# k's first loads on another queue, the first pair's roots on ScalarE and VectorE, the third pair's squares on VectorE

## The chip, the cores and the metric

The kernel runs on one core of a Trainium2 chip. The metric is the device time of one execution in microseconds, the median of the runs made. The engines are TensorE (PE, with its weight loads as PEld), VectorE (DVE), ScalarE (ACT), GpSimd (POOL) and SyncE (SP), which issues most of the loads and stores.

## The reference, cut to what matters

Attention over 8 batches of 12 heads with 448 positions of 64 features, q and k normalised by their root mean square and a gain, then a feed-forward block with a squared ReLU. All data are float32.

```python
def rmsnorm(x, g):
    rms = np.sqrt(np.mean(x * x, axis=-1, keepdims=True) + 1e-06)
    return x / rms * g
q_n, k_n = (rmsnorm(q, g_q), rmsnorm(k, g_k))
scores = 1.0 / np.sqrt(q.shape[-1]) * np.matmul(q_n, k_n.transpose(0, 1, 3, 2))
scores = scores - np.max(scores, axis=-1, keepdims=True)
attn = np.exp(scores)
attn = attn / (np.sum(attn, axis=-1, keepdims=True) + 1e-09)
x = np.matmul(attn, v).transpose(0, 2, 1, 3).reshape(B * S, H * D)
h = x @ w_in
return np.maximum(h, 0.0) ** 2 @ w_out
```

## The kernel before

The heads are taken in pairs, 48 of them. The first twelve pairs are computed alone (`attention_alone`), while the weights of the feed-forward block are read and prepared beside them by VectorE, ScalarE and POOL (`weights`, one small step at a time); after that, attention of later pairs is woven into the matmuls of the feed-forward block. The order of the instructions on each engine is the order in which the program writes them (a manual schedule): every engine runs its own list in order, and waits at an instruction until what it needs is there. No scheduler moves anything. SP likewise issues its transfers in the order of the program, and holds all later ones while it waits for the place of one to come free.

The tile `qk` has eight places of 512 columns, four for the pairs of even number and four for the odd ones. q and k of a pair lie as 112 rows of 4 x 2 x 64 numbers, in two of the four (`places_of`). The other two take the squares. Two pairs later q and k go to one place that held q and to one that held the squares of k.

Each pair of heads needs the reciprocal root of the mean square of each row of q and of k. `normalise_in_turn` does it for the first three pairs, q first and then k: square (L333, ScalarE), sum over 64 columns (L334, VectorE), mean and small constant (L335, VectorE), power of minus one half (L336, POOL). q is then multiplied by its root (L339, VectorE). k isn't: k's roots are the factors of the exponentials later (L820), one per row. For the later pairs `norm` and `roots` do q and k in one, with a logarithm and an exponential on ScalarE (L742, L743) and one Newton step, three small operations on VectorE (L744 to L746), in place of the power.

`first_pair` stands ahead of all. It issues the loads of q (L316, SP), of two small rows of gains (L1588, SP), of k in two loads (L326, SP), and of the gains in columns (L364, POOL), then q and k of the second pair (SP). Ahead of it the table of ScalarE's functions is loaded (L1606). VectorE clears a tile (L377), TensorE runs three matmuls on it (L380) while nothing else is there, and `normalise_in_turn` follows. Between q's and k's part stand the small operations on the gains (`between`: L1591 to L1593, and L373, which multiplies the two gains). TensorE transposes k and q (L385); ScalarE copies k (L387) and scales q by the gains (L389). From L1593 a bound is read by all engines and a branch taken (L1609, L1612); the branch of the whole row maximum isn't taken with these inputs.

In `attention_alone` the first step is: scores of the first pair (L816), exponentials (L820), transposes of the second pair between them (L791, copied at L793 and scaled at L795), first sum (L833), norm of the third pair (`norm(2)`), v of the second pair, first values (L879), load of the fourth pair. Before it stand `load(2)`, two loads of weights (L545) and `norm(1)`. The preparation of the weights has L594 and L611 on ScalarE, L608, L613 and L618 on VectorE, L580 and L588 on POOL. Each scores' matmul needs a bank that the exponentials of the one before left.

Of the kernel before, what the change touches and what calls it, by code (L numbers as in the profile page):

```python
# [10 lines left out]
F32 = mybir.dt.float32  # L11
U32 = mybir.dt.uint32
AF = mybir.ActivationFunctionType
ALU = mybir.AluOpType
# [290 lines left out]
def places_of(qk, i, work):  # L305


    first, second = i % 2 * 4 + work, i % 2 * 4 + 2 + (i // 2 + work) % 2
    return qk[:, first:second + 1:second - first]
# [7 lines left out]
                      q[b, h0:h0 + 2].rearrange("h (p j) d -> p h (j d)", j=4))  # L317


def load_k(nc, qk, k, i):  # L320

    _, H, S, D = k.shape
    b, h0 = divmod(2 * i, H)
    dst = places_of(qk, i, 0)[:S // 4, 1].rearrange("p (j h d) -> p j h d", j=4, h=2)
    for h in range(2):
        nc.sync.dma_start(dst[:, :, h], k[b, h0 + h].rearrange("(p j) d -> p j d", j=4))  # L326


def normalise_in_turn(nc, raw, sq, rstd, mhalf, between=lambda: None):

    SP, _, n = rstd.shape
    for s in range(2):
        nc.scalar.activation(sq[:, s], raw[:, s], AF.Square)  # L333
        nc.vector.tensor_reduce(rstd[:, s], sq[:, s].rearrange("p (n d) -> p n d", n=n), AX, ALU.add)  # L334
        nc.vector.tensor_scalar(rstd[:, s], rstd[:, s], float(n) / sq.shape[2], 1e-6, ALU.mult, ALU.add)  # L335
        nc.gpsimd.tensor_tensor(rstd[:, s], rstd[:, s], mhalf[:SP, 0:n], ALU.pow)  # L336
        if s == 0:
            between()
            nc.vector.tensor_tensor(sq[:, 0].rearrange("p (j h d) -> p h j d", j=n // 2, h=2),  # L339
                                    raw[:, 0].rearrange("p (h j d) -> p h j d", j=n // 2, h=2),  # L340
                                    rstd[:, 0].rearrange("p (h j) -> p h j ()", h=2)
                                    .to_broadcast([SP, 2, n // 2, sq.shape[2] // n]), ALU.mult)
# [7 lines left out]
def first_pair(tc, q, k, g_q, g_k, held):  # L350

    nc = tc.nc
    qk, qkT, ident, mhalf, gains, rstd, bound = held
    D = q.shape[-1]
    S = q.shape[2]
    NJ = 4
    SP = S // NJ
    raw, sq = (places_of(qk, 0, n)[:SP] for n in range(2))
    load_q(nc, qk, q, 0)
    bound[0]()  # L360
    load_k(nc, qk, k, 0)
    for i, g in enumerate((g_q, g_k)):
        for h in range(2):
            nc.gpsimd.dma_start(gains[h * D:(h + 1) * D, i:i + 1], g.rearrange("(d o) -> d o", o=1))  # L364
    load_q(nc, qk, q, 1)
    load_k(nc, qk, k, 1)
    nc.gpsimd.memset(mhalf, -0.5)
    make_identity(nc, ident)


    def between():
        bound[1]()
        nc.vector.tensor_scalar(gains[:, 0:1], gains[:, 0:1], gains[:, 1:2], float(D) ** -0.5, ALU.mult, ALU.mult)  # L373

    with tc.tile_pool(name="ps_first", bufs=1, space=bass.MemoryType.PSUM) as ps_first:

        nc.vector.memset(qkT[:, 1], 0.0)  # L377
        idle = ps_first.tile([2 * D, S], F32, name="idle")
        for _ in range(3):
            nc.tensor.matmul(idle, qkT[:, 1, 0, 0:2 * D], qkT[:, 1, 1], start=True, stop=True)  # L380
        normalise_in_turn(nc, raw, sq, rstd, mhalf, between)
        for s, src in ((1, raw[:, 1]), (0, sq[:, 0])):
            pt = ps_first.tile([2 * D, S], F32, name=f"pt{s}")
            for j in range(NJ):
                nc.tensor.transpose(chunk_of(pt, s, j, NJ), src[:, j * 2 * D:(j + 1) * 2 * D], ident[:SP, :SP])  # L385
            if s:
                nc.scalar.copy(qkT[:, 0, s], pt)  # L387
            else:
                nc.scalar.activation(qkT[:, 0, s], pt, AF.Copy, scale=gains[:, 0:1])  # L389
# [3 lines left out]
def attention_then_ffn_bounded(  # L393
# [73 lines left out]
        turn[0] += n is None  # L467
        return ps_m.tile([P, S], F32, tag="mn"[turn[0] % 2 if n is None else n], name=name)

    qk, qkT, ident, mhalf, gains, rstd0, _ = held  # L470
    gT = consts.tile([P, NFC, 2 * S], F32, name="gT")
    xT = consts.tile([P, 2, NPAIR, S], F32, name="xT")
    xC = consts.tile([P, 3, HC, S], F32, name="xC")
# [247 lines left out]
    def norm(i):  # L721
        if i >= NAT:
            squares(i)
            norm_by_squares(i)
            return scale_by_squares(i)
        raw, sq = (places_of(qk, i, n)[:SP] for n in range(2))
        rstd = rstds[i] = small.tile([SP, 2, 2 * NJ], F32, tag="rstd", name="rstd", bufs=4)
        normed[i] = sq[:, 0], raw[:, 1]
        if i <= 2:
            return normalise_in_turn(nc, raw, sq, rstd, mhalf)  # L730
        nc.scalar.activation(sq, raw, AF.Square)
        nc.vector.tensor_reduce(rstd, sq.rearrange("p s (n d) -> p s n d", d=D), AX, ALU.add)
        nc.vector.tensor_scalar(rstd, rstd, 1.0 / D, 1e-6, ALU.mult, ALU.add)

    def roots(i):


        raw, sq = (places_of(qk, i, n)[:SP] for n in range(2))
        rstd = rstds[i]
        flat = rstd.rearrange("p s n -> p (s n)")  # L740
        y, t = (small.tile([P, 2 * S // 32], F32, tag=tag, name=tag)[:SP, 0:4 * NJ] for tag in ("half", "other"))
        nc.scalar.activation(y, flat, AF.Ln, scale=2.0 ** -63)  # L742
        nc.scalar.activation(y, y, AF.Exp, scale=-0.5, bias=sums["rebias"])  # L743
        nc.vector.scalar_tensor_tensor(t, y, -0.5, flat, ALU.mult, ALU.mult)  # L744
        nc.vector.tensor_tensor(t, t, y, ALU.mult)
        nc.vector.scalar_tensor_tensor(flat, t, 1.5, y, ALU.add, ALU.mult)  # L746
        nc.gpsimd.tensor_tensor(sq[:, 0].rearrange("p (j h d) -> p h j d", j=NJ, h=2),
                                raw[:, 0].rearrange("p (h j d) -> p h j d", j=NJ, h=2),
                                rstd[:, 0].rearrange("p (h j) -> p h j ()", h=2).to_broadcast([SP, 2, NJ, D]),
                                ALU.mult)  # L750
# [735 lines left out]
    with tc.tile_pool(name="words", bufs=2) as spare["pool"]:  # L1486
        load(2)
        for _ in range(2):
            load_w(loaded[0])
            loaded[0] += 1  # L1490
        norm(1)
        with tc.tile_pool(name="first", bufs=2, reuse_waits="tile") as work:

            free = [gT[:, f] for f in range(NFC) if f % HF < HF - 2]
            places[:] = [g.rearrange("p (h q) -> p h q", h=2) for g in free[:2 * NJ]]
            sums[0], sums[1] = (g.rearrange("p (h q) -> p h q", h=2) for g in free[2 * NJ:2 * NJ + 2])
            sums["turned"], sums["factors"] = (g[:, 0:S] for g in free[2 * NJ + 2:2 * NJ + 4])
            sums["ones"] = work.tile([SP, D], F32, tag="ones", name="ones", bufs=1)
            nc.vector.memset(sums["ones"], 1.0)
            sums["rebias"] = work.tile([SP, 1], F32, tag="rebias", name="rebias", bufs=1)  # L1500
            nc.vector.memset(sums["rebias"], -31.5 * math.log(2.0))
            for u, _ in enumerate(attention_alone()):

                weights(min(EARLY, 2 * u + 1, 4 + (EARLY - 4) * u // (4 * NAT - 7)))
                if u == 4 * NAT - 9:
                    load_blocks(5)
        with tc.tile_pool(name="first_product", bufs=2, reuse_waits="tile") as work:
            for u, _ in enumerate(first_product(work, 0)):
                if u == 6:

                    left = ps_s.tile([P, 2, 512], F32, tag="s", name="bits")
                    banks["bits"] = left.rearrange("p a b -> p (a b)")[:, 0:NW].bitcast(U32)
                weights(min(ALL, EARLY + (ALL - EARLY) * (u - 1) // (N1 - 6)))
                if u in (N1 - 16, N1 - 12):
                    load_part(NAT + 2, (u - N1 + 16) // 4)
                if u == N1 - 8:
                    load_v(NAT)
                if u == N1 - 5:
                    norm(NAT + 1)
                if u == N1 - 4:  # L1520
                    transposes(NAT)
                    squares(NAT + 2)
# [39 lines left out]
def kernel(  # L1562
# [27 lines left out]
    def square_of_bound():  # L1590
        nc.vector.tensor_tensor(gg[:, 0, :], gg[:, 0, :], gg[:, 1, :], ALU.mult)  # L1591
        nc.vector.tensor_tensor(gg[:, 0, :], gg[:, 0, :], gg[:, 0, :], ALU.mult)
        nc.vector.tensor_reduce(top, gg[:, 0, :], AX, ALU.max)  # L1593

    held = (
        bound.tile([128, 8, 8 * D], F32, name="qk"),
        bound.tile([128, 2, 2, S], F32, name="qkT"),
        bound.tile([128, 128], F32, name="ident"),
        bound.tile([128, 2 * (S // 32)], F32, name="mhalf"),
        bound.tile([128, 2], F32, name="gains"),  # L1600
        bound.tile([S // 4, 2, 8], F32, name="rstd0"),
        (load_gains, square_of_bound),
    )
    with tc.manual_schedule():

        nc.scalar.preload_act_table_set("natural_log_exp_and_others")  # L1606
        first_pair(tc, q, k, g_q, g_k, held)

    bits = nc.values_load(top.bitcast(mybir.dt.int32))  # L1609
# [37 lines left out]
```

## Time and profile before

| | us |
|---|---|
| median of 3 runs | 1340.4 (1340.37 to 1341.75) |
| profiled execution | 1337.88 |
| its span | 1336.1 |
| TensorE busy from 0 to 10 us | 6.98 |
| TensorE busy from 10 to 20 us | 9.58 |
| TensorE busy from 20 to 30 us | 9.83 |
| TensorE busy from 30 to 40 us | 8.85 |
| ScalarE busy from 10 to 20 us | 9.61 |
| VectorE busy from 10 to 20 us | 5.26 |
| VectorE busy from 20 to 30 us | 9.73 |

The clock that TensorE was granted is 0.998 of full speed. A line of the order of time reads: start in us, busy time in us, engine, line of the kernel, operation, what it writes and reads, size, and in brackets the idle time of the engine ahead of it with what ended that. A line of the chain of waits reads: start, us, what. The chain is followed back from the end, each time to what released the instruction.

### The profile page before, as it was taken

The page shows a single profiled execution, that of the slowest core. Times are in us where ns is not written, and L with a number is a line of the kernel's source. Part 1 is how long each engine was busy: PE and PEld are TensorE (multiplying, and loading weights), DVE is VectorE, ACT ScalarE, POOL GpSimd, SP SyncE. Part 2 cuts the span into 40 slices and gives each one's busy share as a digit, 9 for nine tenths or more (in the row PEclk, how much of TensorE's full clock was granted, in tenths as well). Part 3 has the DMA queues.
Part 4 walks back from the last instruction along what each step waited for, and adds up shares of the span by engine and source line. Part 5 has one row for each costly group of instructions (what it writes and reads, how often), then busy time and mean ns, then how long its engine had stood idle before and what let it go on. Part 6 is the DMA issues. An engine that isn't in the chain of part 4 may idle for free.

```text
span 1336.1 us, 17758 instructions
## 1 busy us (share of the span) xinstructions
PE 1321.4 (99%) x5930; PEld 698.9 (52%) x5930; DVE 855.1 (64%) x1334; ACT 486.2 (36%) x939; POOL 680.1 (51%) x544
## 2 busy tenths in 40 slices
PE   8999999999999999999999999999999999999997
PEld 3333455444446654444444755444444665556887
DVE  6998899489988233467887523457878723336553
ACT  7885656554540012255542011235554101111000
POOL 5677534467656222557774422448675522322452
PEclk9999999999999999999999999999999999999999
DMA  8887999656664433356655433345664444331333
GB/s 222 228 216 190 347 387 330 197 120 136 139 147 119 89 87 88 99 120 134 135 133 144 96 97 88 99 108 114 140 130 129 116 88 145 126 89 48 116 103 57
DMA packets 413817, 190.18 MB, mean 142 GB/s; under 512 B 282388, under 2 KB 408724, under 8 KB 413716
## 3 DMA queue, kind: packets, MB, share of 16 engines
q1 hardware_dynamic: 406164, 180.21, 51.6%
q0 software_dynamic: 4736, 8.40, 2.4%
q8 instruction: 49, 0.80, 0.3%
q10 hardware_dynamic: 2816, 0.34, 0.2%
q14 instruction: 52, 0.43, 0.1%
HBM read 155.72 MB, written 33.16 MB: 141 GB/s over the span
## 4 chain that ended last, share of the span: by engine, by line
PE 90%; DVE 4%; ACT 3%; DMA 1%; issue 1%; POOL 1%; SPq 0%; ACTq 0%; POOLq 0%
PE ps L1204 19%; PE pd L1104 11%; PE pa L1104 10%; PE pc L1104 10%; PE sc L808 7%; PE pav L890 6%; PE pb L1104 5%; PE ps L1387 3%; PE ps L1255 3%; PE pd L1359 2%; PE pc L1359 2%; PE pa L1359 2%; PE sc L816 1%; PE pd L1189 1%; PE pc L1189 1%; PE pa L1189 1%
## 5 line engine op out<-in xcount | busy, mean ns | idle before, releaser
L1076 POOL TENSOR_TENSOR gT<-gT 128x448 f32<-128x448 f32 x96 | 93.7, 978 | 258.5 <-ACT gT L1072 258.5
L773 POOL TENSOR_TENSOR half<-half,mhalf 128x28 f32<-128x28 f32 x36 | 184.8, 5133 | 69.9 <-DVE half L772 60.3
L1204 PE MATMUL ps<-gT,sw 128*128 128x448 f32 x432 | 169.3, 545 | 0.0
L1072 ACT ACTIVATE gT<-gT 128x448 f32<-128x448 f32 x96 | 55.3, 576 | 293.7 <-DVE gT L1120 293.6
L1104 PE MATMUL pa<-xT,sw 128*128 128x448 f32 x384 | 154.9, 539 | 0.0
L1204 PEld LDWEIGHTS ps<-gT,sw 128*128 128x128 f32 x432 | 80.1, 190 | 87.2 <-issue 84.6
L1204 PE MATMUL ps<-gC,sw 128*128 128x448 f32 x288 | 113.1, 546 | 0.0
L808 PE MATMUL sc<-qkT 64*64 64x448 f32 (+1 forms) x1152 | 110.2, 497 | 0.5 <-ACT pr L810 0.2
L1104 PEld LDWEIGHTS pa<-xT,sw 128*128 128x128 f32 x384 | 72.9, 190 | 70.6 <-issue 70.6
L588 POOL TENSOR_TENSOR gC<-gC 128x384 f32<-128x384 f32 x64 | 71.5, 1134 | 59.9 <-DVE gC L584 58.2
L1204 PEld LDWEIGHTS ps<-gC,sw 128*128 128x128 f32 x288 | 53.2, 190 | 59.5 <-issue 58.4
L858 POOL DMA_DIRECT2D xT<-factors x72 | 37.9, 531 | 89.1 <-DMA factors<-square 62.1
L1120 DVE TENSOR_TENSOR gT<-z,pd 128x448 f32<-128x448 f32 x32 | 19.9, 620 | 98.9 <-PE pd L1104 98.7
L810 ACT ACTIVATE pr<-sc 128x896 f32<-128x896 f32 x87 | 76.9, 909 | 11.8 <-PE sc L808 11.8
L775 POOL TENSOR_TENSOR qk<-qk,half 128x448 f32<-128x448 f32 x72 | 77.4, 1096 | 2.8
L1104 PE MATMUL pd<-xT,sw 128*128 128x448 f32 x192 | 77.8, 541 | 0.2
L1104 PE MATMUL pd<-xC,sw 128*128 128x448 f32 x192 | 77.5, 540 | 0.0
L1104 PE MATMUL pc<-xT,sw 128*128 128x448 f32 x192 | 77.4, 539 | 0.0
L1104 PE MATMUL pc<-xC,sw 128*128 128x448 f32 x192 | 77.4, 539 | 0.0
L1104 PE MATMUL pb<-xC,sw 128*128 128x448 f32 x192 | 77.4, 539 | 0.0
L890 PE MATMUL pav<-pr,vt 64*64 64x448 f32 x348 | 72.7, 537 | 0.0
L890 PE MATMUL rest<-pr,vt 64*64 64x448 f32 x348 | 72.7, 537 | 0.0
(282 smaller groups left out, 2447.6 us busy)
## 6 DMA issues: line engine op xcount, KB each, us to landing
sw<-w1s SPq DMA_DIRECT2D x224, 192.0 KB, 2.4
sw<-w2s SPq DMA_DIRECT2D x102, 256.0 KB, 3.4
w1s<-gC SPq DMA_DIRECT2D x8, 1344.0 KB, 7.0
w2s<-gC SPq DMA_DIRECT2D x8, 1344.0 KB, 6.1
qk<-in_q_dram SPq DMA_DIRECT2D x144, 56.0 KB, 2.5
qk<-in_k_dram SPq DMA_DIRECT2D x144, 56.0 KB, 2.3
xT<-factors POOLq DMA_DIRECT2D x72, 112.0 KB, 3.4
words<-in_moe_w_out_dram SPq DMA_DIRECT2D x9, 768.0 KB, 7.1
```

Of the source, the lines that this page charges most:

```text
L588: nc.gpsimd.tensor_tensor(*[blocks_of(n)[:, place_of(n, i)] for i in (dst, x, y)], op)
L773: nc.gpsimd.tensor_tensor(half, half, mhalf, ALU.pow)
L775: nc.gpsimd.tensor_tensor(qkn[:, s], raw[:, s], half[:, s * NG:(s + 1) * NG].rearrange("p g -> p g ()").to_broadcast([P, NG, 32]), ALU.mult)
L808: nc.tensor.matmul(sc[part, h, 0:n], qkT[rows, 0, 1, keys], qkT[rows, 0, 0, of], start=True, stop=True)
L810: nc.scalar.activation(pr, sc[:, :, 0:n], AF.Exp)
L890: nc.tensor.matmul(into, vs[i][rows, h, c, :], probs[i, c][rows, h, :], start=(c == 0), stop=(c == NF), skip_group_check=True)
L1072: nc.scalar.activation(g, src, AF.Relu)
L1076: nc.gpsimd.tensor_tensor(g, g, g, ALU.mult)
L1104: nc.tensor.matmul(ps, stream[n + at][:, c], rhs[:, c], start=first and c == 0, stop=c == HC - 1, skip_group_check=not first)
L1189: nc.tensor.matmul(ps, lhs[:, c], rhs(c), start=start and c == 0, stop=c == HK - 1, skip_group_check=not start)
L1204: nc.tensor.matmul(ps, stream[n][:, c % 4], rhs_of[i][:, c], start=c == 0, stop=c == HF - 1)
L1359: nc.tensor.matmul(ps, lhs[:, c], rhs[:, c], start=first and c == 0, stop=c == HK - 1, skip_group_check=not first)
```

## The change

Five parts:

- the two loads of the first pair's k are issued by ScalarE, as its first instructions, and the load of the function table follows them;
- the first pair's roots are taken by a logarithm and an exponential on ScalarE and a Newton step on VectorE, for q and for k apart, with the squares' own place as room; the product of the two gains (`gain`) stands after both;
- for the third pair, VectorE makes the squares;
- the bias of the exponential, until now set in `attention_alone`, is a column beside the constant of the power, and is set at the start;
- `roots` calls the same two helpers for the later pairs, with the same instructions.

```diff
-def load_k(nc, qk, k, i):
+def load_k(nc, qk, k, i, queue=None):
...
-        nc.sync.dma_start(dst[:, :, h], k[b, h0 + h].rearrange("(p j) d -> p j d", j=4))
+        (queue or nc.sync).dma_start(dst[:, :, h], k[b, h0 + h].rearrange("(p j) d -> p j d", j=4))
+
+def newton(nc, y, t, x):
+
+    nc.vector.scalar_tensor_tensor(t, y, -0.5, x, ALU.mult, ALU.mult)
+    nc.vector.tensor_tensor(t, t, y, ALU.mult)
+    nc.vector.scalar_tensor_tensor(x, t, 1.5, y, ALU.add, ALU.mult)
+
+def first_root(nc, y, x, rebias):
+
+    nc.scalar.activation(y, x, AF.Ln, scale=2.0 ** -63)
+    nc.scalar.activation(y, y, AF.Exp, scale=-0.5, bias=rebias)
+
-def normalise_in_turn(nc, raw, sq, rstd, mhalf, between=lambda: None):
+def normalise_in_turn(nc, raw, sq, rstd, mhalf, between=lambda: None, root=None, by_vector=False):
     for s in range(2):
-        nc.scalar.activation(sq[:, s], raw[:, s], AF.Square)
+        if by_vector:
+            nc.vector.tensor_tensor(sq[:, s], raw[:, s], raw[:, s], ALU.mult)
+        else:
+            nc.scalar.activation(sq[:, s], raw[:, s], AF.Square)
...
-        nc.gpsimd.tensor_tensor(rstd[:, s], rstd[:, s], mhalf[:SP, 0:n], ALU.pow)
+        if root:
+            first_root(nc, sq[:, s, 0:n], rstd[:, s], root)
+        else:
+            nc.gpsimd.tensor_tensor(rstd[:, s], rstd[:, s], mhalf[:SP, 0:n], ALU.pow)
         if s == 0:
             between()
+        if root:
+            newton(nc, sq[:, s, 0:n], sq[:, s, n:2 * n], rstd[:, s])
+        if s == 0:
...
 def first_pair(tc, q, k, g_q, g_k, held):
...
+    load_k(nc, qk, k, 0, nc.scalar)
+    nc.scalar.preload_act_table_set("natural_log_exp_and_others")
     load_q(nc, qk, q, 0)
     bound[0]()
-    load_k(nc, qk, k, 0)
...
-    def between():
-        bound[1]()
+    def gain():
         nc.vector.tensor_scalar(gains[:, 0:1], gains[:, 0:1], gains[:, 1:2], float(D) ** -0.5, ALU.mult, ALU.mult)
...
+        nc.vector.memset(rebias, -31.5 * math.log(2.0))
...
-        normalise_in_turn(nc, raw, sq, rstd, mhalf, between)
+        normalise_in_turn(nc, raw, sq, rstd, mhalf, bound[1], rebias)
+        gain()
...
-            return normalise_in_turn(nc, raw, sq, rstd, mhalf)
+            return normalise_in_turn(nc, raw, sq, rstd, mhalf, by_vector=i == 2)
...
-        nc.scalar.activation(y, flat, AF.Ln, scale=2.0 ** -63)
-        nc.scalar.activation(y, y, AF.Exp, scale=-0.5, bias=sums["rebias"])
-        nc.vector.scalar_tensor_tensor(t, y, -0.5, flat, ALU.mult, ALU.mult)
-        nc.vector.tensor_tensor(t, t, y, ALU.mult)
-        nc.vector.scalar_tensor_tensor(flat, t, 1.5, y, ALU.add, ALU.mult)
+        first_root(nc, y, flat, rebias)
+        newton(nc, y, t, flat)
...
-            sums["rebias"] = work.tile([SP, 1], F32, tag="rebias", name="rebias", bufs=1)
-            nc.vector.memset(sums["rebias"], -31.5 * math.log(2.0))
...
+    powers = bound.tile([128, 2 * (S // 32) + 1], F32, name="mhalf")
...
-        nc.scalar.preload_act_table_set("natural_log_exp_and_others")
         first_pair(tc, q, k, g_q, g_k, held)
```

In the program that results POOL has one more instruction, a reload of its library, right behind the branch and ahead of its first power, which is now the second pair's.

More of the change, by code (lines that the diff above doesn't have):

```diff
@@ L352, in first_pair @@
     nc = tc.nc
-    qk, qkT, ident, mhalf, gains, rstd, bound = held
+    qk, qkT, ident, mhalf, gains, rstd, rebias, bound = held
     D = q.shape[-1]
@@ L468, in bank @@
         return ps_m.tile([P, S], F32, tag="mn"[turn[0] % 2 if n is None else n], name=name)
-    qk, qkT, ident, mhalf, gains, rstd0, _ = held
+    qk, qkT, ident, mhalf, gains, rstd0, rebias, _ = held
     gT = consts.tile([P, NFC, 2 * S], F32, name="gT")
@@ L1598 @@
         bound.tile([128, 128], F32, name="ident"),
-        bound.tile([128, 2 * (S // 32)], F32, name="mhalf"),
+        powers[:, 0:2 * (S // 32)],
         bound.tile([128, 2], F32, name="gains"),
         bound.tile([S // 4, 2, 8], F32, name="rstd0"),
+        powers[:S // 4, 2 * (S // 32):],
         (load_gains, square_of_bound),
```

## The prediction

> **What bounds the kernel now.** I read the page first, then the waits of TensorE over the whole span, then the chain of waits in the first 60 us, then the instructions of the first 31 us in order of time.
>
> ```profile
> span 1336.1 us, 17758 instructions
> PE 1321.4 (99%) x5930; PEld 698.9 (52%) x5930; DVE 855.1 (64%) x1334; ACT 486.2 (36%) x939; POOL 680.1 (51%) x544
> ```
>
> TensorE is busy for 1321.4 of 1336.1 us. All that any change can save on other engines lies in the missing 14.7 us, and the waits of TensorE say where that is:
>
> ```profile
> PE pt L791 <- ACT qkT L793: 2.3, 5, 1.3
> PE idle L380 <- DVE qkT L377: 1.9, 1, 1.9
> PE sc L816 <- ACT qkT L389: 0.8, 1, 0.8
> PE sc L816 <- ACT gT L820: 0.6, 1, 0.6
> ```
>
> The columns are total us, times, longest. Nearly all is in the opening: before the first scores at 8.95 us, and one wait of 1.3 us that ends at 31.15. From 31.15 on TensorE runs almost without gaps (0.21 at 60, 0.61 at 95, 0.21 and 0.22 at 100 and 110), so what the change does to that one moment is handed on to the end. The chain of waits (start, us, what) tells what leads there:
>
> ```profile
> 0.74 2.66 DMA qk<-in_q_dram
> ...
> 5.06 1.68 POOL rstd L336
> ...
> 15.35 1.04 ACT qk L333 x2
> ...
> 21.17 6.37 DMA gT<-in_moe_w_in_dram
> ...
> 28.40 2.19 ACT gT L820 x4
> 30.58 0.43 ACT qkT L793
> 31.01 0.14 issue
> 31.15 0.57 PE pt L791 x4
> ```
>
> So q's load and POOL's power are on it, the third pair's squares (15.35) are, and a weight load that SP issues at 21.17 is. VectorE is not on it from 7.5 to 31 us, but the stage table shows 9.73 of 10 us busy between 20 and 30: it is nearly full there. The order of time gives the prices:
>
> ```profile
> 0.74 1.28 ACT L1606 ACT_TABLE_LOAD   x1 [0.74 <-PEq L1631]
> 1.83 1.38 SPq L326 DMA_DIRECT2D qk<-in_k_dram  x2
> 5.06 1.67 POOL L336 TENSOR_TENSOR rstd<-rstd,mhalf 112x8 f32<-112x8 f32 x1 [0.92 <-DVE rstd L335]
> 6.20 0.63 ACT L333 ACTIVATE qk<-qk 112x512 f32<-112x512 f32 x1 [2.15 <-DMA qk<-in_k_dram]
> 6.76 0.69 DVE L339 TENSOR_TENSOR qk<-qk,rstd 112x512 f32<-112x512 f32 x1 [0.18 <-POOL rstd L336]
> 22.86 0.21 ACT L742 ACTIVATE half<-rstd 112x16 f32<-112x16 f32 x1 [0.46 <-DVE rstd L733]
> 23.11 0.31 ACT L743 ACTIVATE half<-half,rebias 112x16 f32<-112x16 f32 x1
> ```
>
> The last two are the logarithm and exponential of a later pair; its three Newton steps stand at 24.20 to 24.78 on VectorE, 0.58 us together.
>
> [...] q's data moves from 1.8 to 3.0 us with the DMA engines 0.6 to 0.7 busy, so there is room beside it. [...] the first square starts at 3.42, which is 20 ns after q landed and also 1.38 us after the load ended. [...]
>
> **Part 1, k's loads on ScalarE.** The two issues (1.38 us on SP for these very loads) now stand before the table load: 0.74 to 2.12, table load to 3.43. The first square waited for q until 3.42 anyway; I put it at 3.52, with 0.1 us for k's packets beside q's. k itself lands about 1.1 us or more earlier (6.18 before). That buys nothing: TensorE's three warm-up matmuls hold k's transposes until 6.2 to 6.5 whatever lands, and VectorE reduces k only after q's product. On SP the two issues are gone, so q and k of the second pair are issued 1.4 us earlier; nothing waited for those.
>
> **Part 2, roots without POOL, q.** Square 3.52 to 4.15, sum to 4.87, scale to 5.07, logarithm and exponential 5.10 to 5.66 (the three small operations on the gains fill VectorE meanwhile), Newton to 6.26, product from 6.28. Before it was 6.76: 0.5 us won.
>
> **Part 2, k.** Here it is lost again. The order on ScalarE is now: square q, log, exp, square k, log k, exp k, the copy of k's transposes (L387), the scaling of q's (L389), then the second pair's squares. Before, no k root stood ahead of the copy: POOL took it, and it ended at 9.98, beside the second pair's squares, which ended at 10.00. Now k's sum starts at 6.89 behind q's product, its scale ends at 7.78, log 7.81, exp ends 8.37, and only then come the copy to 8.81 and the scaling. That one also waits for the gains' product, which the change moves behind k's Newton steps on VectorE: Newton 8.39 to 8.97, gains to 9.11, scaling 9.13 to 9.76. Before it ended at 8.85. So the first scores start 0.91 us later, and with the second pair's squares behind them (1.15 us) the first exponential starts at 10.99 instead of 10.08. Queued behind the waiting log are those copies and squares; TensorE's first scores wait for them, and SP's load of the third pair's k (8.12 before) waits for k's last Newton step, with two weight loads behind it: about 0.9 us later each.
>
> **Part 3, the third pair's squares on VectorE.** ScalarE loses 1.04 us at 15.35. With the slip its scaling of the second pair ends at 16.25 instead of 15.34, the weight operation L594 follows at once, and the exponentials wait for the scores on TensorE: 17.3 instead of 16.99. Of the slip 0.6 us is regained there. VectorE pays: two products of 0.69 us in its queue. Its add (L833) ends at 15.7, square 16.3, sum and scale 17.2, POOL 18.9, q's product 19.63 (19.22 before); then k's square to 20.23 and k's sum to 20.94, where it was 19.82. VectorE is nearly full from here: the weight operation (19.94 before), the add, and the fourth pair's sum (21.42 before) go to 21.06, 21.53 and 22.55. The logarithm at 22.86, which waited for it, goes to 23.99: plus 1.13. Four exponentials behind it end at 27.5 instead of 26.34. On SP, the load of the fifth pair's k waits for that later k sum, and the weight load behind it (21.17) goes to about 22.25; with its 6.37 us it lands at 28.6. L594 and four exponentials follow, and the transposes of 31.15 start at 32.23.
>
> **Sum.** Plus 0.91 at the first exponential, minus 0.6 by the squares, plus about 0.8 on VectorE: plus 1.1 us at 31 us, and the same at the end. POOL's reload instruction, which the new order needs ahead of its first power, took 0.07 us at most in the trace (3.77 to 3.84); POOL is idle from about 6 to 11.4, so one of up to 5 us would be hidden, beyond that each us counts. The memset and moved bias cost 0.1 us on VectorE beside the loads. Lower end: q lands as before and the weight load takes less than 6.37 with the DMA engines freer; then ScalarE's own queue decides, plus 0.5. Upper end: q lands 0.5 later among k's packets, and VectorE's slip is not caught: plus 2.
>
> The profiled execution took 1337.88 us (span 1336.1 and 1.78 around it). The timed median is 1340.4, 2.5 higher; I add the difference to the median: 1341.5.
>
> **Rivals.**
> A, the table load. [...] With issues at up to 0.81 us each (ScalarE's own at the end of the kernel took 0.32 to 0.81) the first square starts at 5.0 instead of 3.5: 1.5 more on all, 1343.0. [...] From a first square at 5.1 it is slower by more than can be told from no change (0.2%, 2.7 us; three runs spread over 1.4).
> A2, the other side for certain. POOL's reload, the first instruction after the branch there, takes long instead of 0.07 us. At 10 us it ends at 16 instead of 6, and the second pair's power starts at 16 instead of 11.4. TensorE reaches the transposes behind it with 0.4 us to spare, so 4.2 us are added to the forecast: 1345.7. Over the bound from a reload of 7.4 us. For it: the instruction is new there. Against: the same one, for the same library, cost nothing before.
> B, faster. VectorE's two products hide (it is not on the chain of before from 7.5 to 45 us), the squares are worth their full 1.04, and TensorE's four later gaps, 1.25 us in sum, close because ScalarE is ahead: plus 0.91, minus 1.04, minus 1.25 gives minus 1.4, 1339.0. With the 1.3 us gap at 31.15 gone too it would pass 0.2%. For it: the chain. Against: those gaps come when ScalarE and VectorE are both full, and both are shifted with TensorE.
>
> **Chances.** Forecast 0.53, A 0.14, A2 0.05, B 0.28. Of B I put 0.13 beyond 0.2%; slower by more than that are half of A (0.07), A2 (0.05) and the forecast's far upper end (0.05). The range runs from B's outer half to A's value and a little over: 1338.7 to 1343.6. The forecast's own range is 1340.9 to 1342.4.
>
> **What would show it.** First square near 3.5 (A: near 5); q's product near 6.3; end of the scaling of q near 9.8 instead of 8.85; first exponential near 11; the logarithm of the fourth pair near 24; TensorE's wait that ended at 31.15 ending near 32.2. I am wrong if the first scores start before 9 us, or if the fourth pair's logarithm is not later than 22.9.

## The result, and the profile after

| | before | after |
|---|---|---|
| median | 1339.7 us, 22 runs (1338.17 to 1341.75) | 1341.37 us, 22 runs (1339.47 to 1344.24) |
| ratio | | 1.0014, 95% interval 1.0009 to 1.002 |
| profiled execution | 1337.88 us | 1341.18 us |
| span | 1336.1 us | 1339.4 us |

The changed kernel is 1.9 us slower (0.0014 of 1339.7; the interval is 1.2 to 2.7). The predicted time, 1341.5, is met to 0.1 us, but partly by luck: the kernel before ran at 1339.7 beside it and not at 1340.4, so the effect is 1.9 us where 1.1 was predicted.

The page of after, its span and TensorE's line:

```profile
span 1339.4 us, 17768 instructions
PE 1324.0 (99%) x5930; PEld 700.0 (52%) x5930; DVE 858.9 (64%) x1342; ACT 486.4 (36%) x941; POOL 676.3 (50%) x542
```

TensorE's waits, after (total us, times, longest):

```profile
PE sc L837 <- ACT qkT L413: 2.8, 1, 2.8
PE idle L403 <- DVE qkT L400: 1.9, 1, 1.9
PE pt L812 <- ACT qkT L814: 0.7, 3, 0.2
PE sc L837 <- ACT gT L841: 0.6, 1, 0.6
```

The span grew by 3.3 us and TensorE's busy time by 2.6, with the same 5930 matmuls: matmuls became longer. The waits changed places. The one for the first scaled q (L413, L389 before) went from 0.8 to 2.8 us, and the 2.3 us of waits for later transposes fell to 0.7. The chain of waits of after (start, us, what) begins elsewhere too:

```profile
0.74 0.70 ACTq L326
...
1.47 5.23 DMA qk<-in_k_dram
...
7.45 0.70 DVE rstd L350
...
8.43 0.22 ACT qk L338
...
9.38 0.50 issue x2
9.88 0.64 ACT qkT L413
...
10.62 3.33 PE sc L837 x8
13.95 0.94 PE pt L812 x4
14.89 2.62 PE sc L837 x8
```

Before, q's load and POOL's power led to the first scores. Now it is k: its load (landed at 6.70), its sum, its logarithm. From 10.62 to 33.70 us TensorE alone carries the chain. The transposes of the fourth pair's q, which began at 31.15 before, begin at 33.70; this moment is called M below. The order of time of after shows the steps on the way:

```profile
0.74 1.36 ACTq L326 DMA_DIRECT2D qk<-in_k_dram  x2
2.13 1.28 ACT L382 ACT_TABLE_LOAD   x1 [2.13 <-issue]
3.52 0.63 ACT L349 ACTIVATE qk<-qk 112x512 f32<-112x512 f32 x1
6.35 0.69 DVE L361 TENSOR_TENSOR qk<-qk,rstd 112x512 f32<-112x512 f32 x1
6.78 0.63 ACT L349 ACTIVATE qk<-qk 112x512 f32<-112x512 f32 x1 [1.07 <-DMA qk<-in_k_dram]
8.88 0.51 ACT L411 COPY qkT<-pt 128x448 f32<-128x448 f32 x1
9.59 0.21 DVE L395 TENSOR_SCALAR gains<-gains 128x1 f32<-128x1 f32 x1
9.88 0.63 ACT L413 ACTIVATE qkT<-pt,gains 128x448 f32<-128x448 f32 x1 [0.49 <-issue]
12.26 1.67 POOL L355 TENSOR_TENSOR rstd<-rstd,mhalf 112x8 f32<-112x8 f32 x1 [8.11 <-DVE rstd L351]
12.56 1.16 ACT L841 ACTIVATE gT<-sc,rstd 112x448 f32<-112x448 f32 x2 [0.86 <-PE sc L837]
```

q's side is as predicted. k's side isn't, and neither is what follows. The stages of before (stretch, length, busy us of PE, PEld, DVE, ACT, POOL, granted clock, DMA share, GB/s):

```profile
9.00:13.00 4.00, 3.91 (x20) 1.58 (x20) 1.64 (x4) 3.91 (x8) 2.61 (x2) 1.00 0.83 228
13.00:18.00 5.00, 5.00 (x28) 2.10 (x28) 2.61 (x7) 5.00 (x10) 3.63 (x2) 1.00 1.12 314
```

and of after:

```profile
9.00:13.00 4.00, 2.38 (x8) 1.16 (x8) 1.57 (x6) 2.62 (x5) 0.74 (x1) 0.61 0.36 90
13.00:18.00 5.00, 5.00 (x22) 2.16 (x18) 3.93 (x8) 3.59 (x8) 3.36 (x2) 0.63 1.06 335
```

The granted clock was 1.00 there before and is 0.61 and 0.63 now. The first eight score matmuls took 3.33 us instead of 1.76, and the first exponentials (12.56) waited for them. So the 1.67 us by which the first scores are late (10.62 for 8.95) become 4.15 us at the second pair's scores (19.62 for 15.47), of which 1.6 are regained by M, where TensorE no longer waits.

### The profile page after: what moved, and what is told of

Read it like the earlier page. It is cut to its first block, busy times and chain, and to the rows that moved or that the text cites. A ratio compares the mean times of both kernels' runs of the same rounds, so it can differ in the third digit from the quotient of the medians.

```text
span 1339.4 us, 17768 instructions
## 1 busy us (share of the span) xinstructions
PE 1324.0 (99%) x5930; PEld 700.0 (52%) x5930; DVE 858.9 (64%) x1342; ACT 486.4 (36%) x941; POOL 676.3 (50%) x542
## 4 chain that ended last, share of the span: by engine, by line
PE 92%; DVE 3%; ACT 2%; DMA 1%; issue 1%; POOL 0%; SPq 0%; ACTq 0%; DVEq 0%
PE ps L1225 21%; PE pd L1125 11%; PE pc L1125 10%; PE pa L1125 10%; PE sc L829 7%; PE pav L911 7%; PE pb L1125 5%; PE ps L1408 3%; PE ps L1276 2%; PE sc L837 2%; PE pav L900 2%; PE pd L1380 2%; PE pc L1380 2%; PE pa L1380 2%; PE tot L925 1%; PE pd L1210 1%
```

## The experiments

All of them in one table, with before and after: start of k's square (it waits for k's landing), of the first scores, of the second pair's first scores and of M, in us, each from one profiled execution; then the ratio of the times to runs of the kernel before made beside it, with its 95% interval. A ratio rests on 13 to 22 runs of the kernel named (e10: one); a position comes from one execution, so small differences between positions say little.

| run | k's square | first scores | second scores | M | ratio |
|---|---|---|---|---|---|
| before | 6.20 | 8.95 | 15.47 | 31.15 | 1 |
| after | 6.78 | 10.62 | 19.62 | 33.70 | 1.0014 (1.0009 to 1.002) |
| e1_part1 | 6.44 | 9.40 | 15.92 | 31.48 | 1.0006 (0.9997 to 1.0015) |
| e2_part2 | 6.37 | 10.20 | 17.89 | 33.08 | 1.0021 (1.0014 to 1.0029) |
| e3_part3 | 6.30 | 8.89 | 15.42 | 31.31 | 0.9999 (0.999 to 1.0007) |
| e4_fill | 7.22 | 11.06 | 17.57 | 33.17 | 1.0013 (1.0006 to 1.0019) |
| e5_kpool_q | 6.42 | 8.75 | 15.27 | 30.47 | 0.9993 (0.9984 to 1.0001) |
| e6_klate | 6.14 | 8.47 | 15.64 | 31.34 | 1.0007 (0.9998 to 1.0015) |
| e7_kpool_all | 6.95 | 9.09 | 15.85 | 30.94 | 0.9999 (0.9991 to 1.0008) |
| e8_kpool_q3 | 6.08 | 8.50 | 15.10 | 31.27 | 1.0000 (0.9991 to 1.0008) |
| e9_gain | 7.16 | 10.41 | 18.10 | 34.07 | 1.0011 (1.0004 to 1.0018) |
| e10_rows | 5.14 | 9.29 | 16.92 | 33.46 | one run, 1342.23 us |
| e11_cold | 6.36 | 9.40 | 17.90 | 33.09 | 1.0021 (1.0013 to 1.0028) |
| e12_p2fill | 6.35 | 10.19 | 16.69 | 32.51 | 1.0015 (1.0008 to 1.0021) |

M later by 2 us goes with a time about 2 us longer throughout, within about 1.5 us.

### Which part costs: e1, e2, e3

Each takes one part of the change into the kernel before, by the same lines as in the diff of the change: `load_k(nc, qk, k, 0, nc.scalar)` for e1, the roots and the gains' product for e2, `by_vector=i == 2` for e3.

> Part 1 alone (k's loads issued by ScalarE ahead of the table load), the rest as before. Theory C (the loss of the change is TensorE's clock, which fell after it stood idle for 2.8 us): k lands at about 6.7 instead of 6.2, because its packets now share the DMA engines with the second pair's loads, but POOL still takes the roots, TensorE stays idle for under 1.5 us and keeps its clock; time +0.0 to +0.5 us against before. Theory V (the loss is queueing on ScalarE and VectorE, as predicted): also about 0, +0.1. Rival K (late k is the loss): +1 us or more from this part alone.

> Part 2 alone (logarithm, exponential and Newton step for the first pair's q and k), k's loads on SP, third pair's squares on ScalarE. Theory C: the scaling of q ends near 9.8, TensorE idle for about 2 us ahead of the first scores; if that is enough for the clock to fall (granted clock below 0.8 from 9 to 13 us), the first eight score matmuls take about 3.3 us instead of 1.7 and the time is +2 to +4 us; if not, +0.9. Theory V: +0.9 to +1.3 with the clock at 1.00. Rival K: about 0, since k lands as before.

> Part 3 alone (third pair's squares on VectorE). Theory C: no loss, the scores of the second pair's exponentials start up to 0.5 us earlier and the wait that ended at 31.15 ends at 30.5 to 31.2; time -0.7 to 0 us. Theory V: VectorE's queue pushes the fourth pair's logarithm from 22.9 to about 23.5 to 24, and the time is +0.2 to +0.8 us. Rival K: 0.

Part 2 alone costs all of it and perhaps more (1.0021); parts 1 and 3 can't be told from nothing. Rival K, late k as the loss, fails: in e2 k lands nearly as before (its square at 6.37 for 6.20) and the loss is there. In e2 the first scores are 1.25 us late (10.20) behind 2.07 us of idle, and the granted clock is down to 0.79. Part 3 moves work as the prediction said, and its time can't be told from that of before. The chain of waits of e3:

```profile
18.64 0.69 DVE qk L334
...
19.35 0.70 DVE rstd L337
...
22.33 5.38 DMA gT<-in_moe_w_in_dram
...
31.31 0.57 PE pt L794 x4
```

q's part is 0.5 us ahead (its product at 18.03, before at 18.53), the new square of k on VectorE (18.64) takes that and 0.2 more, so the sum starts at 19.35 for 19.14. SP's loads of k wait for that sum, and the weight load behind them starts at 22.33 for 21.17, SP's two issues having taken 2.17 us for 1.23. The load then takes 5.38 us for 6.37 and lands 0.17 us later (27.71 for 27.54). M is 0.16 later although the first scores were 0.06 earlier; both are small for single executions.

### Is it the clock: e4

Three more warm-up matmuls behind q's transposes, so that TensorE isn't idle while it waits; no part of the result changes.

```diff
                 nc.tensor.transpose(chunk_of(pt, s, j, NJ), src[:, j * 2 * D:(j + 1) * 2 * D], ident[:SP, :SP])
+            for _ in range(0 if s else 3):
+                nc.tensor.matmul(idle, qkT[:, 1, 0, 0:2 * D], qkT[:, 1, 1], start=True, stop=True)
```

> The changed kernel with three matmuls on the cleared tile put behind the transposes of the first pair's q on TensorE, the result of which is not used. Theory C: TensorE has no long gap before the first scores, they start at 10.6 as in the changed kernel but run at full clock (8 in 1.7 us instead of 3.3), the transposes that followed at 33.7 come at 31.5 to 32.3, and the time is 1.5 to 2.5 us below the changed kernel, about that of before (0.999 to 1.001). Theory V and rival K: no better than the changed kernel, 1.001 to 1.002 against before, or worse since TensorE has more to do.

The clock stays at 1.00 and the first eight scores take 1.76 us again, but M is only 0.53 us earlier than after, and the time can't be told from after's. k landed at about 7.2 in this execution, and the first scores came at 11.06. So theory C, as stated, is not met: M was to come at 31.5 to 32.3. Counted from the first scores, M comes after 22.11 us, where before has 22.20 and after 23.08: the clock is worth 0.9 to 1.0 us at M, and most of the loss there is the late first scores themselves.

### Is it the order on ScalarE: e5 to e9

e5 keeps the new root for q alone: k's root is POOL's power again, the gains' product stands behind q's product, and parts 1 and 3 are undone.

```diff
-        if root:
+        if root and s == 0:
             first_root(nc, sq[:, s, 0:n], rstd[:, s], root)
...
-        if root:
+        if root and s == 0:
             newton(nc, sq[:, s, 0:n], sq[:, s, n:2 * n], rstd[:, s])
...
-    load_k(nc, qk, k, 0, nc.scalar)
...
+    load_k(nc, qk, k, 0)
...
-        normalise_in_turn(nc, raw, sq, rstd, mhalf, bound[1], rebias)
-        gain()
+        normalise_in_turn(nc, raw, sq, rstd, mhalf, bound[1], rebias, behind=gain)
```

(`behind` is called once, after q's product.) e6 is e5 with k's logarithm, exponential and Newton steps, but written behind the copy and the scaling. e7 is the changed kernel with e5's two edits and with parts 1 and 3 left in. e8 is e5 with part 3 (its ratio, 1.0000, adds nothing to e5's and takes nothing that can be told). e9 is the changed kernel with the gains' product moved and nothing else.

> Part 2 for q alone: q's root by logarithm, exponential and Newton step, k's root by POOL's power as before, the product of the gains right behind q's product; k's loads on SP, third pair's squares on ScalarE. Theory Q (part 2 loses because k's logarithm and exponential stand on ScalarE ahead of the copy of k and the scaling of q): the first scores start at 8.4 to 8.7 us instead of 8.95 (10.2 with part 2 whole), the clock stays at 1.00, the transposes of the fourth pair's q start at 30.5 to 31.1 instead of 31.15, time -0.7 to 0 us against before. Theory R (the new operations themselves cost more than the power on POOL, wherever they stand): half of part 2's loss stays, transposes at 31.9 or later, time +0.7 us or more.

> Part 2 for q and k, with k's logarithm and exponential put behind the copy of k and the scaling of q on ScalarE and its Newton step behind the product of the gains on VectorE; parts 1 and 3 undone. Theory Q: first scores at 8.4 to 8.7, clock 1.00, first exponentials at 10.0 to 10.6 (log and exp take about 0.5 us ahead of the second pair's squares), transposes of the fourth pair's q at 30.8 to 31.6, time -0.4 to +0.5 us. Theory R: as with part 2 whole, transposes near 33.1, time +2 us or more.

> The changed kernel with k's root given back to POOL's power and the product of the gains right behind q's product; k's loads still issued by ScalarE, third pair's squares on VectorE. Theory Q: the first scores start when k has landed (6.7 to 7.2) and ScalarE has squared and copied it: 8.6 to 9.3 us; clock 1.00; transposes of the fourth pair's q at 30.8 to 31.6, time 1.5 to 2.5 us below the changed kernel. Theory R: half of the loss stays, transposes at 32.3 or later.

> As e5_kpool_q, with the third pair's squares on VectorE (parts 2 for q and 3). Theory Q: as e5_kpool_q, first scores 8.4 to 8.7, transposes of the fourth pair's q at 30.3 to 31.1, time -0.9 to 0 us against before. Theory R: transposes at 31.9 or later.

> The changed kernel with one line moved: the product of the gains right behind q's product on VectorE instead of behind k's Newton step. Theory Q gives this about 0.5 us of the first scores' slip (the scaling of q then follows the copy of k at once, near 9.4 instead of 9.88 us); the rest, k's logarithm and exponential ahead of the copy, stays. First scores at 10.0 to 10.3 (k's landing moves this), the clock still falls since TensorE stands idle for over 2 us, transposes of the fourth pair's q at 32.8 to 33.4; time +0.9 to +2 us against before. If the gains alone were the cause, the first scores start below 9.5 and the time is that of before.

e2, its order of time on ScalarE:

```profile
8.02 0.21 ACT L338 ACTIVATE qk<-rstd 112x8 f32<-112x8 f32 x1 [1.02 <-DVE rstd L351]
8.46 0.51 ACT L411 COPY qkT<-pt 128x448 f32<-128x448 f32 x1
9.47 0.63 ACT L413 ACTIVATE qkT<-pt,gains 128x448 f32<-128x448 f32 x1 [0.49 <-issue]
```

and e5:

```profile
6.42 0.63 ACT L349 ACTIVATE qk<-qk 112x512 f32<-112x512 f32 x1 [0.85 <-DMA qk<-in_k_dram]
7.52 0.53 ACT L411 COPY qkT<-pt 128x448 f32<-128x448 f32 x1 [0.47 <-PE pt L409]
8.02 0.63 ACT L413 ACTIVATE qkT<-pt,gains 128x448 f32<-128x448 f32 x1
```

With k's logarithm ahead, ScalarE stands still for 1.02 us in front of it, then for 0.49 in front of the scaling, because the gains' product waits for k's Newton steps. With k's root elsewhere the copy needs only the transposes, and the scaling follows at once: 8.02 for 9.47. The three kernels with the new root for q, k loaded by SP and no k root ahead of the copy (e5, e6, e8) have first scores before 8.8; e7, with k loaded by ScalarE, at 9.09. In e7, which differs from the changed kernel in these two places alone, M is 2.76 us earlier and the time can't be told from that of before, with k landing as late as in after (6.95): that clears late k and part 3 as main causes. But e7 takes k's logarithm off ScalarE altogether. What separates order from work is e6, which keeps all of part 2's operations and moves k's root and the gains: against e2 its first scores are 1.73 us earlier and its M 1.74. So it is the order that makes the first scores and M late. In the time, e6 can't be told from before (1.0007), and its interval overlaps e2's by 0.0001.

e9 separates the gains: from k's square to the scaling it takes 2.51 us (7.16 to 9.67), where after takes 3.10 and e7 1.40 (6.95 to 8.35). So of the 1.7 us the gains' place costs 0.6 and k's root 1.1. e9's M (34.07) is not earlier, against what was expected. k landed 0.4 us later, and a wait of 2.0 us stands ahead of M in that execution, behind which TensorE is slow a second time:

```profile
34.57 2.93 PE L837 MATMUL sc<-qkT 64*112 64x448 f32 x8
```

It was the slowest of e9's 19 runs, so its M isn't typical. e9's time lies between before and after, and can't be told from after's.

e6's first scores are the earliest of all, yet its time is not shorter than that of before: k's logarithm and exponential, now ahead of the second pair's squares, hold those and the exponentials instead (a wait of 0.61 us for an exponential stands ahead of the ninth score matmul). The gain of q's new root is not passed on there. e5's is the best ratio, 0.9993 with an interval that touches 1: not told from before. Its profiled execution has a span of 1339.9 us in spite of an early M; one wait of 2.6 us in the feed-forward block is in it.

### Why k lands late: e10

Part 1 alone, with the second pair's loads issued by SP behind the branch, so that no large load but q's shares the DMA engines with k.

```diff
-    load_q(nc, qk, q, 1)
-    load_k(nc, qk, k, 1)
     nc.gpsimd.memset(mhalf, -0.5)
...
+    load_q(nc, qk, q, 1)
+    load_k(nc, qk, k, 1)
     load_v(0)
```

> Part 1 alone, with the second pair's loads of q and k issued by SP behind the branch (at about 6.3 us) instead of at 2 to 4 us. Theory S (k lands late in the changed kernel because ScalarE's packets share the DMA engines with the second pair's loads, which used to stand behind k in SP's queue): k now lands at 4.5 to 5.3 us. Theory T (loads issued by ScalarE are slower in themselves): k still lands at 6.5 or later. No time is expected from it, the second pair's data come later.

Order of time of e10, ScalarE:

```profile
3.77 0.63 ACT L333 ACTIVATE qk<-qk 112x512 f32<-112x512 f32 x1 [0.35 <-DMA qk<-in_q_dram]
5.14 0.63 ACT L333 ACTIVATE qk<-qk 112x512 f32<-112x512 f32 x1 [0.74 <-DMA qk<-in_k_dram]
```

k is there at 5.1 us, as S expected: 1.1 us earlier than before, which is the head start of the issue. The five other kernels with k on ScalarE start its square between 6.44 and 7.22, the eight with k on SP between 6.08 and 6.42: no overlap, though the nearest two differ by 0.02 only. So the early issue is lost, and more, to the second pair's loads. A row is a queue as the profile lists it; SP's loads are on q1. The page of after shows k's loads on q10, the row of ScalarE's transfers (0.57 MB for 0.34 before). From 4 to 5 us in after, this is what the two rows moved (packets, MB, share of the 16 engines' time):

```profile
q1 hardware_dynamic: 134, 0.13, 39.3%
q10 hardware_dynamic: 203, 0.05, 22.5%
```

Both rows move at once. From 4 to 6 us the DMA engines are 0.74 busy in after and 0.20 in e10 (199 GB/s for 39). On one row the second pair's loads stood behind k: in before its q, issued at 3.25 us, landed 3.8 us later, at 7.05, and k at 6.18. On two they run beside it: in after that q, issued at 2.06, landed 4.4 us later, at 6.46, ahead of k at 6.70. The order of single packets is not shown. The whole time of e10 says nothing of part 1, since the second pair comes later in it.

### What a slow TensorE costs: e11, e12

e11 is the kernel before with one warm-up matmul instead of three; no part of the result changes. The half clock that it prices is that of after, where 0.50 was granted from 10.6 to 14.0 us.

```diff
-        for _ in range(3):
+        for _ in range(1):
```

> The kernel before with one warm-up matmul on TensorE instead of three, whose result is not used; nothing else is changed. It prices the half clock by itself: the first scores start as before at 8.9 to 9.1 us, but at a granted clock of 0.5 to 0.7 from 9 to 13 us. Theory C1 (the clock costs about 0.7 to 1 us in all, the rest of the time is hidden by ScalarE's queue): transposes of the fourth pair's q at 31.8 to 32.3 instead of 31.15, time +0.5 to +1.3 us. Theory C2 (the clock is the main loss of the changed kernel): transposes at 33 or later, time +1.7 us or more.

Order of time of e11, TensorE:

```profile
7.65 0.98 PE L385 MATMUL pt<-ident,qk 112*128 112x112 f32 x4 [0.27 <-DVE qk L339]
9.40 3.33 PE L816 MATMUL sc<-qkT 64*112 64x448 f32 x8 [0.77 <-ACT qkT L389]
```

The first scores are 0.45 us later than before and take 3.33 us; M comes at 33.09, 1.9 later, and the time is 2.8 us longer (1.7 to 3.8): C2's side. So a slow TensorE alone can cost as much as the whole change. Counted from the first scores, a slow TensorE cost 1.5 us at M here, and 0.9 in after. That left open whether e4 had undervalued the clock, so the edit of e4 was made on part 2 alone, where k lands at the usual time.

> Part 2 alone as in e2, with three more warm-up matmuls behind q's transposes; no part of the result changes. In e2 the first scores started at 10.20 behind 2.07 us of idle, the first eight took 2.27 us at a granted clock of 0.79, and the transposes of the fourth pair's q stood at 33.08. C, the clock is a term of its own: the first scores stay at 10.2 (within 0.3), the first eight take 1.76, the granted clock is 1.00 from 9 to 18 us, and the transposes stand 22.2 us behind the first scores as before, at 32.4 (within 0.3); time 1.0009 to 1.0018 of before, below e2's 1.0021. P, the placement alone sets the loss (another engine or a load holds the later stages, and what a warm TensorE gains is given back in a wait): the first eight take 1.76, and the transposes stay at 33.0 to 33.3, time 1.0018 or more.

Order of time of e12, TensorE:

```profile
7.58 2.43 PE L411 MATMUL idle<-qkT 128*128 128x448 f32 x6
10.19 1.76 PE L839 MATMUL sc<-qkT 64*112 64x448 f32 x8 [0.17 <-ACT qkT L415]
32.51 0.57 PE L814 MATMUL pt<-ident,qk 112*128 112x112 f32 x4 [1.44 <-ACT qkT L816]
```

The first scores start where they did in e2 (10.19), the clock reads 1.00 from 9 to 18 us, and M comes 22.3 us behind them, as C expected. Against e2, M gains 0.57 us; the ratios, 1.0015 and 1.0021, have overlapping intervals. The second scores gain 1.20 us (16.69 for 17.89), and half of it is given back in the wait ahead of M (1.44 for 0.79 us): a warm TensorE reaches that wait sooner. So at M the clock is a term of its own, smaller there than where it arises, and the placement remains the larger. In the time of e4 and e12 the gain of a warm TensorE is not shown; only e11 shows in the time what a slow one costs.

## Why the prediction was right, and where it was not

**What bounds the kernel.** One reading was wrong. Of TensorE's 14.7 us that aren't busy, 4.8 lie ahead of 31.15 us, about 2 between there and the last matmul, and 8.0 behind that (it ends at 1328.1 of 1336.1). So the opening held a third of it, not nearly all. The argument needed only that the opening's waits reach the end.

**Part 1.** The first square is at 3.52, the predicted value to the digit, with the two issues at 1.36 us and the table load ending at 3.41. The digit is chance: in the other five kernels with these loads the square waits for q and starts at 3.58 to 3.77. Rival A put 1.38 us between the end of the table load and the first square, about what stands there in before (1.40 us). That the load causes it was not shown, since the square of before also stands 0.02 us behind q's landing. The rival is refuted: in after the square follows the load by 0.11 us. "k itself lands about 1.1 us or more earlier" failed: in after it landed 0.5 us later, and e10 shows why. "That buys nothing" held for gains, but a loss was not considered: the forecast saw room beside q, and not the second pair's loads beside k.

**Part 2, q.** Product at 6.35 for 6.28: right.

**Part 2, k.** The mechanism was right, and e5, e6, e7 and e9 show it: the copy and the scaling stand behind k's logarithm, and the gains behind k's Newton steps. The size was 0.91 us, and 1.67 was measured. k's sum started at 7.45 instead of 6.89, 0.56 us, nearly all of it because of the landing; the remaining 0.2 is in the hand-overs between ScalarE and VectorE, each a little longer than taken (0.08 us ahead of the logarithm and of the scaling, for 0.03 and 0.02), and in the gains' product (0.21 for 0.14).

**What was missing.** The sum had no term for TensorE's clock. Behind 2.8 us of idle the first eight score matmuls took 3.33 us in after, for 1.76 before; e4 and e12 put the clock at 0.9 and 0.6 us at M. It also shows in the first exponential, forecast near 11: it started at 12.56, after ScalarE had waited 0.86 us for the slow score matmuls.

**Part 3.** Alone, it behaved as worked out: minus 0.6 and plus 0.8 is plus 0.2, and from the first scores to M e3 has 22.42 us for 22.20. VectorE's part of it is met: k's sum was to be 1.12 us late, 0.91 of it the slip, which e3 doesn't have, and is 0.21 late there. In the changed kernel the fourth pair's logarithm came at 25.82, not 23.99, and this no longer mattered: TensorE was later still.

**Sum.** At M plus 1.67 and plus 0.88 is 2.55 (33.70 for 31.15), where 1.1 was predicted; 1.9 us are left in the time. The profiled executions don't show where the rest was regained (from M to the end, after has 1305.7 us and before 1304.95); single executions of one kernel differ by more than that, and it stays open. The predicted direction and bound held: slower, by less than 0.2%. That the time was met to 0.1 us is luck: late k and the slow TensorE were left out, and M came 1.45 us later than forecast. About 0.65 of that was regained in a way that isn't explained, and 0.7 was hidden by a median of before lower than the one that the forecast was added to.

**Rivals.** A2 is refuted: POOL's power at 12.26 waited for VectorE alone, after 8.11 us of idle. B's claim that VectorE's products hide is not borne out by e3, where they push k's sum and the weight load behind it. Its other claim, that TensorE's later waits close, came true for another reason: TensorE was slower, not ScalarE ahead.

## What to carry to other kernels

An operation that is moved off a slow engine (POOL's power took 1.67 us here) must not land in front of work that another engine waits for: count what stands behind its wait in the new queue, here a copy and a scaling behind a logarithm that the result needed only later (1.1 us of the first scores' slip). Before a load is moved to another issuer for a head start, look at what it preceded on its old queue: here k was first there, and on two rows its square started at 6.44 to 7.22 us, for 5.14 with the second pair's loads out of the way. When a change lengthens an idle time of TensorE, add slower matmuls behind it as a term of its own: here eight score matmuls took 2.27 to 3.33 us for 1.76, and that was worth 0.6 (e12) to 1.5 us (e11) at M.

## What the runs showed of the hardware

- Idle times of 2.07 us (e2), 2.0 us (e9) and 2.8 us (after) ahead of the first scores were followed by a lower granted clock of TensorE: 0.79, 0.77 and 0.61 from 9 to 13 us. So was the 2.0 us ahead of e9's M (0.94 from 31 to 60 us, with eight score matmuls in 2.93 us at 34.57). A single idle time of 1.44 us (e12, ahead of M) was not: eight took 1.76 us at 33.02. But e10 has 1.39 and 0.77 us with one group of transposes between them, and a clock of 0.58. In these runs the length of one idle time doesn't decide.
- Counted from the last matmul that is no transpose to the next one, the stretch ahead of the first scores was 3.94 (after), 3.67 (e9), 3.46 (e2) and 3.12 us (e10) where the clock fell, and at most 2.70 (e1) where it stayed (e11 left out, whose record shows no fall). e9's M, with 2.52 and a fall, doesn't fit, so no fixed threshold comes out of these runs.
- The granted clock in the records doesn't show every slow stretch. e11's stages:

```profile
0.00:9.00 9.00, 3.82 (x10) 1.82 (x10) 3.88 (x10) 3.41 (x5) 5.31 (x13) 1.00 0.54 132
9.00:13.00 4.00, 3.60 (x10) 1.51 (x11) 1.19 (x3) 2.83 (x6) 2.66 (x2) 1.00 0.76 216
```

It reads 1.00 while eight score matmuls take 3.33 us, the very time that they took in after at 0.61. The first warm-up matmuls show it too: in e12 five records of 128x448 take 3.94 us from 2.79 on, at a recorded 1.00, and six of the same size 2.43 us from 7.58 on. In these runs the duration of a known matmul is the surer sign.
